# Filter planes of 289 columns loaded in long runs with the negation on VectorE, the first two gate and up chunks split into token halves, and the second block's norms moved into the down stage

## The chip, the cores and the metric

One core of a Trainium2 chip. The metric is the device time of one execution in microseconds (us). "Span" is the length of the profiled execution, which in most runs is some 1.8 us shorter than its time. Engines: PE is TensorE's matmul, PEld its weight load, DVE is VectorE, ACT is ScalarE, POOL is GpSimd, SP is SyncE, which issues most transfers.

## The reference, cut to what matters

```python
x = A_x                                            # 2048 tokens x 576, bf16
X = rfft2(layernorm(x)) * (w_r + 1j * w_i)         # filter planes w_r, w_i: 2048 x 289
h = x + irfft2(X).astype(bf16)
n = layernorm(h)
out = h + (gelu(n @ w_gate) * (n @ w_up)) @ w_down # 576 -> 4608 -> 576
```

The transforms are done as matrix products with tables. The tokens are worked on in 16 tiles of 128; the feed-forward part takes four blocks of four tiles. A "chunk" is 128 of the 4608 hidden columns; each has 18 matmuls of 512 tokens (gate and up).

## The kernel before: what the change and the argument touch

The two filter planes come in 36 loads, 32 of them of 16 partitions, all of one plane first. GpSimd makes the negated imaginary plane, then clears VR. VectorE multiplies the spectrum YS by both planes at once.

```python
def w_loads(pl, hf, eng):                    # column 0 of 289 is skipped: runs of 288
    ...
    for jj in range(4):
        o.append((WS[jj:64:4, g0:g1, 1 + pl, :], 1 + (16 * jj + g0) * K2, [[128 * K2, 16], [K2, g1 - g0], [1, K2 - 1]], jj))
        ...
for f in w_loads(1, 0, SP) + w_loads(1, 1, SP) + w_loads(0, 0, SP) + w_loads(0, 1, SP):
    f()
...
for i in range(NG):                          # 16 pieces of 288 columns on GpSimd
    P.op(POOL, lambda v, g=GORD[i]: v.tensor_scalar(WS[:, g, 0, :], WS[:, g, 2, :], -1.0, 1.0, ...), ...)
    if i == NVZ:
        P.op(POOL, lambda g: g.memset(VR[:, :, :, :, :], 0.0), w=["Vz"])
...
P.op(DVE, lambda v: v.tensor_tensor(TP[:, sl, :, :, q0:q1], y4, w4, op=ALU.mult), ...)   # the product
```

The last eight token tiles are inverse transformed late, inside the down stage of block 0 ("deferred tiles"). One such tile is a matmul group, an eviction EB on ScalarE, four VectorE operations (QB, YB), two matmuls on YB, and then:

```python
def def_n(c):
    for h in range(2):
        P.op(PE, ... ITD[:, c - NPRE, :], YB[:, 288 * h:288 * h + 288] ...)
    P.op(DVE, ... scalar_tensor_tensor(x2, banks(4, 2, 288), 1.0, x2, ..., accum_out=SB2[:, 0, c:c + 1]), ...)  # update of XO
    square(c, JD[:, :], "JD")                # ScalarE, sum of squares for the norm

def down(tb, p):
    for h, (d0, d1) in enumerate(((0, cut), (cut, D))):
        cd = NPRE + 2 * p + h if tb == 0 else NT
        if cd < NT:
            def_i(cd)                        # a deferred tile every 36 matmuls
        for f in ...:
            if cd < NT and f == 22:
                def_n(cd)
            ... matmul of down ...
```

The statistics, norms and DMA transposes of token block 1 are emitted during gate and up of block 0:

```python
if tb == 0 and f == 8:
    ln2_m(2); ln2_r(2); ln2_q(2); ln2_c(2)   # mean, variance, square root, reciprocal
f0, f1 = (15, 3) if tb == 0 else (2, 4)
if tb < 3 and f >= f0 and (f - f0) % f1 == 0 and (f - f0) // f1 < 4:
    norm(...); turn_dma(...)
```

## Time and profile before

| | before |
|---|---|
| time, 3 runs ahead of the prediction | 496.44 us (496.36 to 496.98) |
| span of the profiled run | 494.9 us |
| filter stage, first matmul to first inverse matmul | 19.98 to 52.44 us |
| gate and up of block 0 start | 64.77 us |
| down of block 0 starts (first deferred tile's matmul) | 134.81 us |
| gate and up of block 1 start | 176.16 us |

Read it by stages: from 64.77 us on PE has no gap worth a name, so the time can only fall by what is won ahead of that point, and any new wait after it is paid in full. The prediction shows the profile lines for this. (Its table cuts the down stage at 134.88 us, at the stage's second matmul; below I count from the first, at 134.81.)

### The profile page before, as it was taken

Reading aid. Unit: us, or ns where it says so; the run is one execution under the profiler, and the core shown is the slowest. Engines: PE = TensorE matmul, PEld = TensorE weight load, DVE = VectorE, ACT = ScalarE, POOL = GpSimd, SP = SyncE. Lnnn points to the kernel's source line nnn. Section 1 sums busy time; section 2 is a strip of 40 time slices with the busy share of each in tenths; the row PEclk is TensorE's granted clock in tenths of the full one; section 3 lists DMA queues with packets and bytes.
Section 4 is the critical chain, followed back from the end, with each engine's and each line's share of the span. In section 5 each row is a group of like instructions: output and inputs, shape, how many; then the busy total and the mean of one; then the engine's idle time right before and its main releaser. Section 6 shows DMA issues by size and latency. Waiting matters only on the chain.

```text
span 494.9 us, 9880 instructions
## 1 busy us (share of the span) xinstructions
PE 486.1 (98%) x4338; PEld 288.1 (58%) x4338; DVE 192.4 (39%) x418; ACT 158.9 (32%) x300; POOL 34.6 (7%) x53
## 2 busy tenths in 40 slices
PE   7999999999999999999999999999999999999998
PEld 3767655555588854444477744444677544444775
DVE  6679743444365644433311144333211233333111
ACT  6989865232312243232300033232100132233000
POOL 5750701000000010000000000000000000000000
DMA  8666898411000062000000001000000000000000
GB/s 276 163 188 215 277 350 275 178 25 27 4 13 13 19 191 60 19 9 1 1 13 19 18 15 23 19 1 1 7 19 12 14 1 1 1 1 2 12 19 19
DMA packets 27164, 31.26 MB, mean 63 GB/s; under 512 B 11664, under 2 KB 20112, under 8 KB 27120
## 3 DMA queue, kind: packets, MB, share of 16 engines
q1 hardware_dynamic: 24224, 18.68, 13.0%
q0 software_dynamic: 2896, 11.95, 7.1%
q8 instruction: 34, 0.56, 0.5%
q14 instruction: 10, 0.08, 0.1%
HBM read 26.28 MB, written 2.36 MB: 58 GB/s over the span
## 4 chain that ended last, share of the span: by engine, by line
PE 88%; DVE 4%; issue 1%; ACT 0%; DVEq 0%
PE PS L824 57%; PE PS L874 29%; DVE TP L594 1%; DVE VR L565 1%; PE PS L841 1%; PE PS L684 1%; PE PS L723 1%; DVE ZS L600 1%; DVE XO L726 0%; PE PS L855 0%; DVE ZR L603 0%; PE PS L610 0%; DVE HN L757 0%; PE PS L777 0%; DVE TM L734 0%
## 5 line engine op out<-in xcount | busy, mean ns | idle before, releaser
L824 PE MATMUL PS<-HT,WG 64*128 64x512 bf16 x2106 | 228.5, 376 | 0.0
L824 PEld LDWEIGHTS PS<-HT,WG 64*128 64x128 bf16 x2106 | 107.3, 94 | 119.8 <-issue 1.0
L833 ACT ACTIVATE GL<-PS 128x512 bf16<-128x512 f32 x144 | 85.9, 597 | 257.3 <-PE PS L824 243.4
L834 DVE TENSOR_TENSOR AT<-GL,PS 128x512 bf16<-128x512 bf16 x144 | 98.9, 687 | 175.0 <-ACT GL L833 175.0
L874 PE MATMUL PS<-WD,AT 128*128 128x288 bf16 (+2 forms) x1152 | 144.3, 286 | 0.0
L874 PEld LDWEIGHTS PS<-WD,AT 128*128 128x128 bf16 x1152 | 110.8, 98 | 30.7 <-ACT GL L833 1.3
L877 DVE TENSOR_TENSOR OS<-PS,XO 128x288 bf16<-128x288 f32 (+2 forms) x32 | 14.6, 457 | 100.3 <-PE PS L874 100.3
L824 PE MATMUL PS<-HT,WGX 64*128 64x512 bf16 x486 | 53.4, 376 | 0.0
L824 PEld LDWEIGHTS PS<-HT,WGX 64*128 64x128 bf16 x486 | 23.7, 94 | 28.8
L714 ACT ACTIVATE JD<-XO 128x576 bf16<-128x576 bf16 x8 | 5.5, 683 | 28.5 <-DVE XO L858 28.5
L594 DVE TENSOR_TENSOR TP<-YS,WS 128x1152 bf16<-128x1152 bf16 (+2 forms) x17 | 11.8, 715 | 6.8 <-DMA WS<-in_A_w_r_dram 6.7
L574 PE MATMUL PS<-FT,U 128*128 128x288 bf16 x96 | 14.1, 286 | 0.1
L565 ACT ACTIVATE CUS<-PS 128x576 bf16<-128x576 f32 x16 | 13.5, 862 | 0.5 <-PE PS L574 0.4
L565 ACT ACTIVATE YS<-PS 128x576 bf16<-128x576 f32 x16 | 11.3, 705 | 2.3 <-DVE TP L594 2.2
L520 PE MATMUL PS<-ATS,XO 128*128 128x128 bf16 (+1 forms) x128 | 10.1, 221 | 1.7 <-POOL XN L534 1.1
L584 PE MATMUL PS<-CUS,BT 128*128 128x288 bf16 x64 | 10.5, 286 | 1.2 <-ACT YS L565 0.9
L464 DVE BATCH_NORM_STATS2 ST<-XO 128x6 f32<-128x288 bf16 x24 | 9.3, 438 | 4.5 <-DMA XO<-in_A_x_dram 4.5
L574 PEld LDWEIGHTS PS<-FT,U 128*128 128x128 bf16 x96 | 9.1, 98 | 2.9 <-ACT CUS L565 0.4
L520 PEld LDWEIGHTS PS<-ATS,XO 128*128 128x128 bf16 (+1 forms) x128 | 7.4, 97 | 4.7 <-POOL XN L534 1.6
L610 PE MATMUL PS<-VT,ZS 128*128 128x256 bf16 x64 | 9.0, 273 | 1.1 <-DVE VR L565 0.5
L565 ACT ACTIVATE V<-PS 128x512 bf16<-128x512 f32 (+1 forms) x17 | 10.0, 639 | 0.3 <-PE PS L610 0.2
L757 DVE TENSOR_SCALAR HN<-XO,TM,RS 128x576 bf16<-128x576 bf16 (+1 forms) x32 | 10.0, 361 | 0.0
(77 smaller groups left out, 215.0 us busy)
## 6 DMA issues: line engine op xcount, KB each, us to landing
WD<-in_B_w_down_dram POOLq DMA_DIRECT2D x9, 576.0 KB, 21.4
WG<-in_B_w_gate_dram POOLq DMA_DIRECT2D x4, 1152.0 KB, 9.7
WG<-in_B_w_up_dram SPq DMA_DIRECT2D x4, 1152.0 KB, 7.9
out_dram<-OS SPq DMA_DIRECT2D x30, 72.0 KB, 1.6
XO<-in_A_x_dram SPq DMA_DIRECT2D x3, 576.0 KB, 7.4
WGX<-in_B_w_gate_dram POOLq DMA_DIRECT2D x1, 1152.0 KB, 6.9
WGX<-in_B_w_up_dram SPq DMA_DIRECT2D x1, 1152.0 KB, 10.8
HT<-HN SPq DMA_TRANSPOSE x60, 2.4
```

What stands on the lines that cost most here:

```text
L464: P.op(DVE, lambda v, c=c, h=h: v.bn_stats(ST1[:, c, h, :], XO[:, c, 288 * h:288 * h + 288]), r=[("X", c)], w=[("ST1", c, h)])
L520: P.op(PE, lambda t, b=b, lhs=lhs, p0=p0, p1=p1, s=s, e=e, o=o, c=c: t.matmul(bank(b, p0, p1, o, o + 128), lhs, ATS[:, c, :], start=s, sto ...
L565: fn = (lambda v: v.tensor_copy(dst, src)) if eng == DVE else (lambda a: a.activation(dst, src, ACTF.Copy))
L574: P.op(PE, lambda t, b=b, m=m, us=us, o=o, g=g: t.matmul(bank(b, 0, 128, 0, 2 * HK), U[:, us, g, :, :], FT[:, 3 * o + (2 if us == 4 else u ...
L584: P.op(PE, lambda t, b=b, tb=tb, m=m, s3=s3, sp_=sp_: t.matmul(bank(b, 0, 128, 0, KW), BT[:, sp_, tb, :], CUS[:, s3, m, :], start=(m == 0) ...
L594: P.op(DVE, lambda v: v.tensor_tensor(TP[:, sl, :, :, q0:q1], y4, w4, op=ALU.mult), r=[("Y", sl), ("Wn", i)] + wkeys[0 if 1 <= g < 9 else ...
L757: P.op(eng, lambda v, c=c, hs=hs, o0=o0, o1=o1, x0=x0, x1=x1: v.tensor_scalar(HN[:, hs, o0:o1], XO[:, c, x0:x1], TM[:, 1, c:c + 1], RS2[:, ...
L824: op = P.op(PE, lambda t, h0=h0, kt=kt, wt=wt, b=b, s=(not second and j == 0), e=(second and j == n - 1): t.matmul(bank(b), wg_tile(slot)[ ...
L833: P.op(ACT, lambda a: a.activation(GL[:, s2, :], bank(b0), ACTF.Gelu_apprx_tanh), r=[("PS", b0)], w=[("GL", s2)])
L834: P.op(DVE, lambda v: v.tensor_tensor(AT[:, f, :], GL[:, s2, :], bank(b0 + 1), op=ALU.mult), r=[("GL", s2), ("PS", b0 + 1)], w=[("AT", f)])
L874: P.op(PE, lambda t, b=b, d0=d0, d1=d1, f=f, p=p: t.matmul(bank(b, 0, 128, 0, d1 - d0), AT[:, f, 128 * p:128 * p + 128], WD[:, f, d0:d1], ...
L877: P.op(DVE, lambda v, b=b, d0=d0, d1=d1, p=p, c=c: v.tensor_tensor(OS[:, p % 2, d0:d1], bank(b, 0, 128, 0, d1 - d0), XO[:, c, d0:d1], op=A ...
```

## The change

Its intent: start the filter products earlier (fewer and longer loads, both first halves ahead of the second halves, negation taken off GpSimd), and fill the end of the inverse stage with the first two gate and up chunks, split in two token halves of 256 columns. It also re-deals the evictions of the filter stage between VectorE and ScalarE, and moves the statistics, norms and transposes of block 1 into the down stage of block 0, where the deferred tiles now come every 28 matmuls.

```diff
+    def w_up(pl, hf):                       # one load of 64 partitions, whole runs
+        P.dma(SP, WS[0:64, 1 + pl, g0:g1, :].rearrange("p g k -> p (g k)"), bass.AP(src, g0 * K2, [[128 * K2, 16], [16 * K2, 4], [1, (g1 - g0) * K2]]), ...)
+    def w_down(pl, hf):                     # four loads of 16 partitions, rows of 289
+    for pl in (1, 0):
+        w_up(pl, 0)
+        w_down(pl, 0)
...
+    for pl in (1, 0):
+        w_up(pl, 1)
+        w_down(pl, 1)
...
-        w3 = WS[:, g, :, q0:q1]
+        w3 = WS[:, 1, g, 1 + q0:1 + q1]     # row pitch 289: every second row starts off 4 bytes
...
+    def st_w(i):                            # negation, 4 pieces of 1156 columns
+            P.op(DVE, lambda v, g0=g0, g1=g1: v.tensor_scalar(WS[:, 0, g0:g1, :], WS[:, 2, g0:g1, :], -1.0, None, op0=ALU.mult), ...)
...
-    for i in range(NG):
-        P.op(POOL, ... tensor_scalar(WS[:, g, 0, :], WS[:, g, 2, :], -1.0, 1.0, ...
-        if i == NVZ:
-            P.op(POOL, lambda g: g.memset(VR[:, :, :, :, :], 0.0), w=["Vz"])
+    P.op(POOL, lambda g: g.memset(VR[:, :, :, :, :], 0.0), r=[("ATS", c) for c in range(NT)], w=["Vz"])
...
+    def gu_first(i):
+        for a in range(4):
+            gu_part(a % 2, a > 1, *PARTS[i])        # PARTS = ((0, 256), (256, 512))
...
+    for j, c in enumerate(range(NPRE, NT)):
+        defer(DSTEP * j, def_i, c)                  # DSTEP, DLAG = 28, 24
+        defer(DSTEP * j + DLAG, def_n, c)
+    t2 = DSTEP * (8 - NPRE) + DLAG
+    defer(t2, ln2, 3)
+    for c in range(4, 8):
+        defer(t2 + 12 + DSTEP * (c - 4), turn, c)
...
-            if tb == 0 and f == 8:
-                ln2_m(2) ...
-            f0, f1 = (15, 3) if tb == 0 else (2, 4)
-            if tb < 3 and f >= f0 ...
+            f0, f1 = 2, 4
+            if 0 < tb < 3 and f >= f0 ...
```

The order of the filter stage and of the inverse stage is a string of tokens in the kernel; both strings are new (the inverse one ends "... z2 N7 z3 G0 G1", where G0 and G1 are the two token halves).

## The prediction

> **What bounds the kernel now.** I read the page's busy shares first, then the table by stretches, then the waits and the timelines of the two stages the change touches, and last the chain of work.
>
> ```profile
> PE 486.1 (98%) x4338; PEld 288.1 (58%) x4338; DVE 192.4 (39%) x418; ACT 158.9 (32%) x300; POOL 34.6 (7%) x53
> PE   7999999999999999999999999999999999999998
> ```
> The matmul engine is busy 98% of the span. That is an average, so I cut it by stage:
>
> ```profile
> 20.00:52.44 32.44, 29.66 (x238) 21.75 (x236) 25.10 (x65) 29.23 (x52) 12.00 (x19) 1.00 0.58 171
> 52.44:64.77 12.33, 11.82 (x100) 8.61 (x101) 9.92 (x34) 10.19 (x24) 7.91 (x11) 1.00 1.02 364
> 64.77:134.88 70.11, 70.11 (x649) 36.62 (x650) 27.42 (x51) 26.94 (x46) 1.28 (x2) 1.00 0.42 135
> 134.88:176.16 41.28, 41.28 (x368) 33.51 (x368) 23.66 (x57) 9.99 (x26) 0.00 (x0) 1.00 0.05 14
> ```
> The columns are stretch, length, then busy time of PE, weight load, DVE, ACT, POOL. From 64.77 us on (gate/up, then down of the first token block) PE has no gap: that time only moves if work is added or a wait appears. Only what lies before 64.77 can be won: the filter stage (20.00 to 52.44) and the inverse stage (52.44 to 64.77).
>
> In the filter stage PE's own work is about 27.6 us: 160 matmuls of 288 columns at 0.122 us start to start (six in 0.735 us), 64 of 256 columns at 0.109, ten small ones. So some 4.8 us of its 32.4 are waits. The waits and the timelines name the source:
>
> ```profile
> DVE TP L594 <- DMA WS<-in_A_w_r_dram: 6.7, 1, 6.7
> 18.16 2.40 DVE L529 CAST U<-PS 128x384 bf16<-128x384 f32 x5
> 27.26 1.43 DVE L594 TENSOR_TENSOR TP<-YS,WS 128x1152 bf16<-128x1152 bf16 x2 [6.70 <-DMA WS<-in_A_w_r_dram]
> 6.76 12.71 SPq L218 DMA_DIRECT2D WS<-in_A_w_i_dram  x18
> 19.51 12.57 SPq L218 DMA_DIRECT2D WS<-in_A_w_r_dram  x18
> ```
> VectorE ends its last forward eviction at 20.56 and stands still until 27.26, when the real filter plane lands. SyncE issues 36 filter loads one after another, 0.70 us each; the eighth real one is issued at about 25.1. After 27.26 VectorE runs nearly without gaps until the last filter product is summed at 51.2, and the chain of work runs through it. So the filter stage is a VectorE chain that a late load starts late.
>
> [...] 36 loads of 36 to 72 KB hold SyncE for 25.3 us. [...] With 289 columns and a start at column 1, every second filter row starts off a 4-byte boundary. The trace of before has no such case[...]. [...]
>
> **The change part by part.**
>
> *Loads.* Half of each plane now goes in one load of 64 partitions with long runs, the rest in four. The first half of both planes is 10 loads instead of 16 and comes before the second halves. It is issued from 6.23 us, at up to 0.7 us each to about 13. Bytes: before has moved x, tables and 1.26 MB of filter only when 4.8 MB are through; at the 203 and 272 GB/s of the stretches 0-7 and 7-20 us that is about 19.5 us. So the wait of 6.7 us goes.
>
> *VectorE chain.* It is now first held by data: forward matmuls at 20.0, evictions, second matmul, eviction of YS. By hand with the trace's durations (CUS 0.86, YS 0.70, four matmuls 0.5) the first product starts at 23.9 instead of 27.26: 3.4 us earlier. Work of VectorE from there to the end: 15 products at 0.68 and a split one 0.75 (11.0), 16 pairs of sums at 0.44 (7.0), seven VR casts at 0.43 (3.0), 2.5 V evictions taken over from ScalarE (about 1.6), the second half of the negations. These are 1156 columns; rows of 128 and 576 columns took 0.25 and 0.42 us, so by that slope about 0.65 each, 1.3 here; the first two run while VectorE would wait. Sum 23.9, before 22.7 in 23.9 with gaps. With the same gaps of 1.2 us the inverse stage starts near 49.2, before 52.44: **3.2 us**. ScalarE loses 2 CUS, 1 YS and 2.5 V evictions and gains VR casts, about 25.4 us from 21.07, and PE 27.6 from 20.0: both end before 49, but close, so I expect no more.
>
> *Inverse stage.* Its matmuls are 48 and 32 at 0.122 and 20 at 0.055, 10.9 us in 12.33. The two gate/up chunks cost 3.9 us (18 matmuls at 0.108 each; half as wide and twice as many when split). Before, they came after: 12.33 + 3.9 = 16.2 us. Now the first token half runs while the last two tiles are still being transposed and evicted, and three of four norms are on POOL. I expect 15.4: **0.8 us**.
>
> *Normalisation of block 1.* The second-block norms, their square root and the transposes move from gate/up of block 0, where they were hidden, into its down stage, and the deferred inverse tiles come every 28 matmuls instead of 36. Here is one such tile before:
>
> ```profile
> 138.47 0.76 DVE L858 SCALAR_TENSOR_TENSOR XO<-PS,XO 128x576 bf16<-128x576 f32 x1 [0.59 <-PE PS L855]
> 139.27 0.68 ACT L714 ACTIVATE JD<-XO 128x576 bf16<-128x576 bf16 x1 [3.40 <-DVE XO L858]
> 140.43 0.41 ACT L844 ACTIVATE EB<-PS 128x288 f32<-128x288 f32 x1 [0.39 <-PE PS L841]
> 140.88 0.82 DVE L848 TENSOR_TENSOR QB<-PS,EB 128x288 f32<-128x288 f32 x2 [0.23 <-ACT EB L844]
> 142.11 0.45 DVE L851 TENSOR_TENSOR YB<-QB 128x288 bf16<-128x288 f32 x1
> 143.18 0.41 PE L855 MATMUL PS<-YB,ITD 128*128 128x288 bf16 x2
> 176.15 1.28 ACT L744 ACT_TABLE_LOAD   x1
> ```
> In program order the steps form a ring: update of XO (L858) to square 0.80, square to the next ScalarE operation 0.68, EB to QB 0.45, QB to the end of the second YB 1.68, then the next update 0.49 after it: 4.10 us. Before, PE took 5.16 us per tile and never waited. At 28 matmuls it takes 28 x 0.1225 + 0.75 = 4.18: the slack is 0.08 us. Into that ring come (a) once, after the first tile, the table load (1.28) and square root (0.3) ahead of the next EB: 1.5 us of PE waiting; (b) in three tiles a norm (0.55) and an output eviction (0.38) between YB and the update: 0.93 in place of 0.49 us, less the slack, 0.36 each, 1.1 in all. **PE loses about 2.5 us** here. The transposes (20 at about 1.3 us on SyncE) start some 10 us into the stage of about 44 and end near 40: no wait, with 3 to 4 us to spare.
>
> Sum: -3.2 - 0.8 + 2.5 = -1.5, so 494.9 us.
>
> **The rivals.** *A, the front gain arrives whole and the down stage costs nothing* (492.4): for it speaks that PE had no gap there before and that ScalarE and VectorE are far from full (9.99 and 23.66 of 41.28 us); against it the ring above, which is latency, not load. [...] *C, another wait takes the place of the removed one*: the 1.26 MB land later than 23.9, because the load of x and tables fills the queue (DMA share 0.87 from 7 to 20 us); each microsecond of delay is one of gain lost, up to 496.5 at 2 us. *D, transposes late*: if each took 2 us the second block would wait some 10 us, about 505; the longest landing seen was 5.8 us against a median of 2.4. One in fifty.
>
> **Range and chances.** The front gain may be 2.5 to 5 us, the cost in the down stage 0 to 3.5; A and C mark the ends, which gives 492.2 to 497.2. Two per cent is 9.9 us: there are not 9.9 us of waits ahead of 64.77 to remove, and only D would add as many.
>
> **What would show it.** Right: the first product at about 24 us, with no DMA wait of microseconds ahead of it; the first inverse matmul near 49; the third gate/up chunk (first full-width matmul of 512 columns) near 64.5, before 68.7; products of odd and even rows equally long, about 0.75 us; in the down stage PE waits for YB in the second tile (1.5 us) and in three more, and the stage takes about 43.8 us for 41.28. Wrong: products of two lengths; PE without a gap in that stage (then 492 to 493); or a wait of the first gate/up chunk of block 1 for the transposes.

-3.2 - 0.8 + 2.5 makes -1.5, which takes 496.4 us to 494.9.

## The result, and the profile after

Ratios below are the mean time of one kernel's fast runs over that of the other's fast runs of the same rounds, so not quite the ratio of the medians quoted beside them.

Before 496.55 us (median of 4 runs, 496.36 to 496.98), after **495.90 us** (495.74 to 496.05). Ratio 0.9986, 95% interval 0.9968 to 1.0003: the same within 2%, and a gain of about 0.65 us that the interval does not set apart from none. The control run later, `after_again`, gave 495.91 us beside 496.45 us.

The page of the kernel after, head lines: the busy share of PE is 98% as before, and the slices show no gap either. Such a page cannot tell where a microsecond went.

```profile
span 494.2 us, 9935 instructions
PE 485.8 (98%) x4374; PEld 285.1 (58%) x4374; DVE 193.8 (39%) x421; ACT 153.3 (31%) x300; POOL 31.3 (6%) x43
PE   7999999999989999999999999999999999999998
```

So to the table by stretches of the kernel after (stretch, length, then busy time of PE, weight load, DVE, ACT, POOL, clock, DMA share, GB/s):

```profile
19.78:50.87 31.09, 29.69 (x242) 22.54 (x240) 29.49 (x71) 26.68 (x52) 5.59 (x7) 1.00 0.61 176
50.87:61.88 11.01, 10.81 (x95) 8.25 (x96) 8.66 (x31) 9.39 (x23) 4.58 (x8) 1.00 1.04 369
61.88:131.96 70.08, 70.08 (x686) 33.20 (x685) 23.94 (x38) 25.20 (x45) 7.40 (x11) 1.00 0.39 129
131.96:175.53 43.57, 42.05 (x371) 33.31 (x370) 25.67 (x69) 10.76 (x27) 1.32 (x2) 1.00 0.20 57
```

The second cut, 50.87 us, lies 0.9 us behind the first inverse matmul, so the first two rows are not to be set against those of the prediction's table; the milestones below can be compared. Gate and up (the third row) still have PE busy from end to end. The down stage (the fourth row) does not any more: 42.05 busy of 43.57. By milestones, in us from the span's start:

| milestone | before | after | gained so far |
|---|---|---|---|
| first matmul of the filter stage | 19.98 | 19.78 | 0.20 |
| first filter product | 27.26 | 24.41 | 2.85 |
| first inverse matmul | 52.44 | 49.98 | 2.46 |
| first matmul of the second inverse step | 53.97 | 51.81 | 2.16 |
| first gate and up matmul | 64.77 | 61.88 | 2.89 |
| first matmul of down, block 0 | 134.81 | 131.96 | 2.85 |
| first gate and up matmul, block 1 | 176.16 | 175.53 | 0.63 |

The front won 2.9 us, and the down stage gave 2.2 of them back: 41.35 us became 43.57. The first 0.20 us are not shown to be the change's: the first filter matmul starts at 19.98 us here and at 19.40 in `before_down_new`, which has the same front. Counted from that matmul, the front won 2.7 us.

The timeline of the kernel after around the start of the filter products (start, us, engine, line, operation, count, and in brackets the idle time and its releaser):

```profile
5.70 3.35 SPq L222 DMA_DIRECT2D WS<-in_A_w_i_dram  x5
9.09 3.17 SPq L222 DMA_DIRECT2D WS<-in_A_w_r_dram  x5
...
16.73 4.35 SPq L222 DMA_DIRECT2D WS<-in_A_w_r_dram  x6
...
17.97 2.40 DVE L534 CAST U<-PS 128x384 bf16<-128x384 f32 x5
18.11 3.52 POOL L648 MEMSET VR<- 128x4096 bf16 x1 [0.84 <-DVE ATS L499]
20.29 2.02 DVE L609 TENSOR_SCALAR WS<-WS 128x1156 bf16<-128x1156 bf16 x2
...
24.41 1.43 DVE L604 TENSOR_TENSOR TP<-YS,WS 128x1152 bf16<-128x1152 bf16 x2
```

The first halves of both planes are issued by 12.3 us, and the wait of 6.7 us on a load ahead of the first product is gone: no bracket stands on that line. But the first two negations take 2.02 us together. Drawn singly, the first takes 1.66 us, and one that runs later 0.46. It began at 20.29 us, while GpSimd was still clearing VR (18.11 to 21.63), and it ended 0.3 us after the clearing did.

The products of the kernel after, all instructions of that tile (durations in ns: shortest, median, longest):

```profile
L604 DVE TENSOR_TENSOR TP<-YS,WS x17: 223/755/764, 24.4 to 48.1; 128x1152 bf16<-128x1152 bf16 x15, 128x1024 bf16<-128x1024 bf16 x1, 128x128 bf16<-128x128 bf16 x1
```

There is one length of product, not two: 755 ns in the median and 764 at most, with every second row off a 4-byte boundary; before, with no such row, the median was 750. So the products of two lengths that the prediction lists under "Wrong" did not come.

The timeline of the kernel after in the down stage, from the end of the first deferred tile to the third:

```profile
136.66 0.68 ACT L731 ACTIVATE JD<-XO 128x576 bf16<-128x576 bf16 x1 [3.63 <-DVE XO L879]
137.44 1.28 ACT L761 ACT_TABLE_LOAD   x1
138.73 0.30 ACT L761 ACTIVATE RS<-RS,EPT 128x4 f32<-128x4 f32 x1
138.94 0.39 ACT L865 ACTIVATE EB<-PS 128x288 f32<-128x288 f32 x1
139.36 0.82 DVE L869 TENSOR_TENSOR QB<-PS,EB 128x288 f32<-128x288 f32 x2
...
141.10 0.42 PE L876 MATMUL PS<-YB,ITD 128*128 128x288 bf16 x2 [1.35 <-DVE YB L872]
...
145.37 0.64 DVE L774 TENSOR_SCALAR HN<-XO,TM,RS 128x576 bf16<-128x576 bf16 x2
145.51 0.42 PE L876 MATMUL PS<-YB,ITD 128*128 128x288 bf16 x2
145.91 0.45 DVE L917 TENSOR_TENSOR OS<-PS,XO 128x288 bf16<-128x288 f32 x1
146.28 0.75 DVE L879 SCALAR_TENSOR_TENSOR XO<-PS,XO 128x576 bf16<-128x576 f32 x1
```

ScalarE's operations start here in the order of the program: square (JD) at 136.66 us, table load at 137.44, square root (RS) at 138.73, which is 1.29 us after the load's start, and then, at 138.94, the eviction EB that everything waits for. PE stands at 141.10 until YB comes. The starts of L876 in this run are 135.41, 141.10, 145.51, 149.91, 154.32, 158.51, 162.68 and 166.86 us, that is periods of 5.69, 4.41, 4.40, 4.41, and then 4.17 to 4.19, which is PE's own work (28 x 0.1225 + 0.75 = 4.18). So PE waits 1.5 us once and 0.23 us three times: 2.2 us. The waits of the weight load, which stands idle a little longer than PE, name the same place, in the sum over the run (us in total, times, longest):

```profile
PEld PS L876 <- DVE YB L872: 2.7, 4, 1.7
```

### The profile page after: what moved, and what is told of

The parts are those of the page before. It is cut to its first block, busy times and chain, and to the rows that moved or that the text cites. A ratio compares the mean times of both kernels' runs of the same rounds, so it can differ in the third digit from the quotient of the medians.

```text
span 494.2 us, 9935 instructions
## 1 busy us (share of the span) xinstructions
PE 485.8 (98%) x4374; PEld 285.1 (58%) x4374; DVE 193.8 (39%) x421; ACT 153.3 (31%) x300; POOL 31.3 (6%) x43
## 4 chain that ended last, share of the span: by engine, by line
PE 87%; DVE 8%; ACT 2%; DMA 1%; issue 1%; SPq 0%; DVEq 0%
PE PS L824 57%; PE PS L914 26%; DVE ST L469 1%; DMA XO<-in_A_x_dram 1%; PE PS L701 1%; PE PS L585 1%; DVE TP L604 1%; PE PS L595 1%; DVE U L534 1%; PE PS L740 1%; DVE QB L869 1%; ACT JD L731 1%; DVE XO L879 1%; PE PS L862 0%; DVE ZS L615 0%
## 5 line engine op out<-in xcount | busy, mean ns | idle before, releaser
L824 PE MATMUL PS<-HT,WG 64*128 64x512 bf16 (+1 forms) x2142 | 228.5, 372 | 0.0
L824 PEld LDWEIGHTS PS<-HT,WG 64*128 64x128 bf16 x2142 | 103.9, 94 | 122.9 <-issue 0.7
L576 ACT ACTIVATE YS<-PS 128x576 bf16<-128x576 f32 x15 | 9.7, 662 | 2.5 <-PE PS L595 2.2
L869 DVE TENSOR_TENSOR QB<-PS,EB 128x288 f32<-128x288 f32 x16 | 6.6, 452 | 7.0 <-ACT EB L865 6.8
L576 ACT ACTIVATE CUS<-PS 128x576 bf16<-128x576 f32 x14 | 9.1, 655 | 0.6 <-PE PS L585 0.4
L510 PE MATMUL PS<-ZD 128*128 128x512 bf16 x20 | 7.4, 534 | 1.5 <-POOL ZD L409 1.5
```

The lines of the kernel that those rows point to most:

```text
L576: fn = (lambda v: v.tensor_copy(dst, src)) if eng == DVE else (lambda a: a.activation(dst, src, ACTF.Copy))
L824: op = P.op(PE, lambda t, h0=h0, kt=kt, wt=wt, b=b, s=(not second and j == 0), e=(second and j == n - 1): t.matmul(bank(b, 0, 128, c0, c1) ...
L869: P.op(DVE, lambda v, i=i, op=op: v.tensor_tensor(QB[:, 2 * i:2 * i + 2, :], o2, e2, op=op), r=["EB", ("PS", 3)], w=[f"Q{i}"])
```

## The experiments

Twelve runs were made, one of them the changed kernel again, each timed in five rounds against the kernel before (medians 496.49, 496.39 and 496.45 us in the three groups). All gave correct results. Theory: the front gain is real and smaller than planned, and the down stage loses some 2 us in a ring of dependences that goes through ScalarE and VectorE in program order. Rivals: the loss is VectorE's load and not the order; the front gain comes from something else than the earlier loads.

### The down stage

**down_old**: the changed kernel, with the down stage, norms and transposes of the kernel before.

```diff
-DSTEP, DLAG = 28, 24
+DSTEP, DLAG = 36, 22
-    defer(t2, ln2, 3)
-    for c in range(4, 8):
-        defer(t2 + 12 + DSTEP * (c - 4), turn, c)
+            if tb == 0 and f == 8:
+                ln2(3)
-            f0, f1 = 2, 4
+            f0, f1 = (15, 3) if tb == 0 else (2, 4)
```

> The changed kernel with the second block's statistics, norms and transposes put back into the gate/up stage of the first block, and the deferred tiles every 36 matmuls as before. Ring theory (the 2.3 us lost in the down stage come from the table load and the norms in the ring of the deferred tiles): the down stage goes from 43.57 back to 41.3 us, PE has no wait for YB, total about 493.6 us. Rival (the down stage is longer because something else of the change, such as the front's later weight loads, disturbs it): stays near 43.5, total 495.9.

493.85 us (493.71 to 494.05), ratio to before 0.9948 [0.9935, 0.9960]; it is faster than both kernels. Down of block 0 starts at 131.93 us, as in the changed kernel, and gate and up of block 1 at 173.30: a stage of 41.37 us instead of 43.57, with no wait for YB. The whole loss sits in what was moved there and in the closer spacing, which this run puts back together.

**before_down_new**: the opposite, the kernel before with the new down stage only (DSTEP and DLAG 28 and 24, the square root, norms and transposes of block 1 after its first deferred tile).

> The kernel before with only the down stage of the changed kernel: statistics, norms and transposes of the second block in the down stage, deferred tiles every 28 matmuls. Ring theory: down stage about 43.6 instead of 41.28 and nothing else changed, total about 498.8, clearly slower than before. Rival (the cost needs the changed front): 496.5.

498.61 us (498.36 to 499.16), ratio 1.0046 [1.0034, 1.0058]. The stage runs from 134.29 to 177.87 us, 43.58 us. The loss of 2.2 us does not depend on the front.

**sqrt_early**: the changed kernel with the statistics and the square root of block 1 alone put back into gate and up; norms, transposes and the spacing of 28 stay.

```diff
-    defer(t2, ln2, 3)
+            if tb == 0 and f == 8:
+                ln2(3)
```

> The changed kernel with only the square root of tiles 4 to 7 (its statistics are ready early) put into the gate/up stage; norms and transposes stay in the down stage, deferred tiles every 28 matmuls. Ring theory: the 1.5 us wait of the second deferred tile goes, the three waits of about 0.2 us stay; down stage about 42.1, total about 494.4. Rival (VectorE is simply loaded too much by the norms): the long wait stays, total 495.9.

494.50 us (494.38 to 494.67), ratio 0.9960 [0.9947, 0.9974]. L876 now starts at 135.45, 139.63, 143.95, 148.36, 152.77 and 156.95 us: the long wait is gone, and three of 0.14 to 0.23 us stay. The stage takes 41.97 us, so the table load and the square root cost 1.6 of the 2.2 us, the norms and output evictions the other 0.6.

**square_late**: the changed kernel with one instruction moved: the square of a deferred tile is emitted four matmuls into the next tile, behind that tile's EB, instead of ahead of it. All the work stays in the stage.

```diff
-        square(c, JD[:, :], "JD")
+        defer(DSTEP * (j + 1) + 4, square, c, JD[:, :], "JD")
```

> The changed kernel with the square of each deferred tile emitted after the next tile's EB instead of before it; same work on every engine. Ring theory (ScalarE's order puts the square and the table load between update and EB): the square leaves the ring (0.7 us) and the table load runs ahead of the wait, so the down stage falls to 41.3 to 41.8, total about 493.8. Rival (load of VectorE): the same work in the same time, nothing changes, 495.9.

494.19 us (493.77 to 494.61), ratio 0.9953 [0.9940, 0.9965]. Its timeline:

```profile
132.66 0.41 ACT L865 ACTIVATE EB<-PS 128x288 f32<-128x288 f32 x1
133.09 1.28 ACT L761 ACT_TABLE_LOAD   x1
...
135.45 0.41 PE L876 MATMUL PS<-YB,ITD 128*128 128x288 bf16 x2
...
137.17 0.30 ACT L761 ACTIVATE RS<-RS,EPT 128x4 f32<-128x4 f32 x1 [2.81 <-DVE RS L756]
...
139.63 0.41 PE L876 MATMUL PS<-YB,ITD 128*128 128x288 bf16 x2
```

With no square in front of it, the table load runs in idle time, at 133.09 us, four microseconds ahead of the square root that needs it. L876 then comes every 4.17 or 4.18 us throughout, and the stage takes 41.35 us, exactly that of the kernel before. VectorE still does every norm and eviction there; had its load been the cause, nothing would have changed. The rival falls, and the cause is the order on ScalarE: the square between the update of XO and the next EB closes the ring. Whether the old spacing of 36 matmuls alone, with all the work left in the stage, would also have been enough no run here shows.

**norm_pool**: the changed kernel with the four norms on GpSimd, which shortens VectorE's part of the ring.

```diff
     def turn(c):
-        norm(c)
+        norm(c, POOL)
```

> The changed kernel with the four norms of the second block in the down stage on POOL instead of VectorE. Ring theory: the 1.5 us wait for the table load stays, the three waits of about 0.2 us go; down stage about 42.9, total about 495.2. Rival (load of VectorE is the cause): nearly the whole 2.3 us goes, total about 493.7.

495.79 us (495.56 to 496.08), ratio 0.9987 [0.9974, 0.9999]: I had expected 495.2 and missed. The stage takes 43.34 us. Two of the three short waits are gone, as expected, and the long one stays; but the first short one grew from 0.23 to about 0.4 us. The timeline of this run shows where:

```profile
139.35 6.47 POOL L774 TENSOR_SCALAR HN<-XO,TM,RS 128x576 bf16<-128x576 bf16 x8 [57.10 <-DVE RS L765]
...
144.31 0.95 DVE L871 TENSOR_TENSOR YB<-QB 128x288 bf16<-128x288 f32 x1
```

All of GpSimd's norms run in one go (139.35 to 145.82 us), and one YB beside them took 0.95 us instead of 0.46. The other three YB operations in that stretch took 0.45 to 0.46, so why this one was longer is not shown.

### The front

**loads_old**: the changed kernel with 36 loads, one plane after the other as before (but of 289 columns; the VT table's load moves ahead of them).

```diff
-    for pl in (1, 0):
-        w_up(pl, 0)
-        w_down(pl, 0)
...
+    for pl in (1, 0):
+        w_loads(pl, 0)
+        w_loads(pl, 1)
```

> The changed kernel with the filter planes loaded as before: 36 loads of 16 partitions (289 columns), imaginary plane whole, then real plane, all after VT. Load theory: the first product waits for the real plane until about 27.2 us instead of 24.4; the matmul engine loses what it cannot make up, inverse stage about 2 us later, total about 498. Rival (the front gain comes from sharing evictions between engines, the loads were not the limit): within 0.5 us of the changed kernel, 495.9 to 496.4.

498.04 us (497.23 to 499.14, 6 runs), ratio 1.0035 [1.0022, 1.0047]. The wait for the load is back in its timeline:

```profile
25.61 1.43 DVE L599 TENSOR_TENSOR TP<-YS,WS 128x1152 bf16<-128x1152 bf16 x2 [1.36 <-DMA WS<-in_A_w_r_dram]
```

The first product comes 1.2 us later than with the new loads (25.61 against 24.41), and gate and up start at 63.08 instead of 61.88. That is earlier than the 27.2 us I had expected for the product, and the wait is 1.36 us and not 6.7: VectorE, which now does some of the evictions ahead of the product, is ready for it at 24.25 us and not at 20.56, and the eighth load of the real plane is issued at 23.11 us instead of 24.00. The profiled run was the fastest of the six; the others' spans were 0.4 to 2.0 us longer. So the new loads are worth 1.2 us in the profile and 2.1 in the medians. The run puts number, shape and order of the loads back together; which of them counts it does not tell.

**neg_pool**: the changed kernel with the negation back on GpSimd, in 16 pieces ahead of VR's clearing.

```diff
+    for i in range(NG):
+        P.op(POOL, lambda v, g=GORD[i]: v.tensor_scalar(WS[:, 0, g, :], WS[:, 2, g, :], -1.0, 1.0, ...), ...)
...
-            st_w(i)
```

> The changed kernel with the negation on POOL again (16 pieces, as before), all else as changed. If moving the negation to VectorE was needed for the gain: total about 496.5 or more, because POOL's pieces are late. My theory (the negation was not on the path; the loads were): first product about 23 to 24.4, total within 0.5 us of the changed kernel, 495.4 to 496.2.

498.50 us (497.11 to 498.88), ratio 1.0034 [1.0023, 1.0046]: missed, I had expected no harm. The first product comes at 23.98 us, as expected, but gate and up start at 62.94. The timeline:

```profile
23.48 6.01 POOL L649 TENSOR_SCALAR WS<-WS 128x289 bf16<-128x289 bf16 x8 [1.08 <-DMA WS<-in_A_w_i_dram]
...
27.29 1.90 DVE L604 TENSOR_TENSOR TP<-YS,WS 128x1152 bf16<-128x1152 bf16 x2
```

Eight pieces that GpSimd did in 4.08 us just before (beside evictions out of PSUM) take 6.01 beside VectorE's products, and two products take 1.90 instead of 1.43. In all, three products and four of the sums beside GpSimd's pieces are longer than in the changed kernel, together by 1.45 us. They all lie between the first product, 0.43 us earlier than in the changed kernel, and the fifth, 0.99 later (29.95 against 28.96), and the delay then stays at about 1.0 to the first inverse matmul (51.02 against 49.98). Beside GpSimd's clearing the products were not longer: in the kernel before, VR's clearing (26.65 to 30.17 us) lay beside the first products, and those took 1.43 us for two; so did two in neg_pool itself (at 31.50 us, beside the clearing of 29.55 to 33.07). In the kernel before, GpSimd's pieces ran from 18.39 to 26.6 us, while VectorE mostly waited for its load (20.56 to 27.26), so no product lay beside them. Why pieces and products take longer side by side no run here shows. Once the loads are early, the negation is better off GpSimd, at least in this order of work (495.90 us against 498.50). The profiled run was the fastest of the five (the other spans were 0.7 to 1.8 us longer), and what the others lost besides is not shown.

**memset_late**: the changed kernel with VR's clearing behind the first two negations.

```diff
-    P.op(POOL, lambda g: g.memset(VR[:, :, :, :, :], 0.0), r=[("ATS", c) for c in range(NT)], w=["Vz"])
...
+            if i == 0:
+                P.op(POOL, lambda g: g.memset(VR[:, :, :, :, :], 0.0), r=[("Wn", 0), ("Wn", 4)], w=["Vz"])
```

> The changed kernel with POOL's zeroing of VR (3.5 us) after the first two negations on VectorE instead of beside them. [...] (the first negation took 1.66 us against 0.46 for the same shape later because it waits until POOL's memset ends at 21.6): the first two negations take about 0.46 each, the first product starts about 1.2 us earlier (23.2 instead of 24.4), total 0.3 to 0.8 lower (the matmul engine is nearly the limit of the stage), about 495.4. Rival (the negation is slow because of the loads landing or the odd start of the rows): 1.66 again, total 495.9.

495.94 us (495.52 to 496.15), ratio 0.9991 [0.9978, 1.0004]. The timeline:

```profile
19.86 0.82 DVE L609 TENSOR_SCALAR WS<-WS 128x1156 bf16<-128x1156 bf16 x2
20.74 3.52 POOL L653 MEMSET VR<- 128x4096 bf16 x1 [3.91 <-DVE WS L609]
```

Both negations together take 0.82 us instead of 2.02: the 1.2 us are gone once the clearing runs behind them. With the clearing beside it the first negation had ended at 21.95 us, 0.3 after the clearing (21.63), so it looks like a wait for the clearing's end; what makes it wait is not shown. The stage as a whole gains less, 0.4 us: from the first filter matmul to the second inverse step 31.64 us, against 32.03. And the time does not move at all. In this run, and in the two below that hold the same edit, the time exceeds the span by 2.0 to 2.1 us, against 1.7 to 1.9 in every other run. Something outside the profiled span takes back what the span gains; the runs do not tell what, and I leave it open.

**no_split**: the changed kernel with the first two chunks whole and after the inverse stage.

```diff
-... N6 p0 p3 A0 z2 N7 z3 G0 G1""".split()
+... N6 p0 p3 A0 z2 N7 z3""".split()
```

> The changed kernel, but with the first two gate and up chunks whole and after the inverse stage, as in the kernel before; everything else stays. Theory (the halves placed inside the inverse stage fill its short waits on evictions, worth some 0.7 us): about 496.5 us, and the third full-width chunk of block 0 about 0.6 us later than in the changed kernel (near 66.4 us from the span's start). Rival (the split only moves the same TensorE work and fills nothing): 495.9 us and the third chunk at 65.8 us.

496.60 us (496.36 to 496.94), against 495.91 for the changed kernel in the same group (`after_again`). Down starts at 132.53 us instead of 131.80, 0.73 later. From the second inverse step to gate and up it takes 10.83 us, as before (10.80), against 10.07 when split. Two lines tell what the split fills, the first gate and up matmuls of no_split, then those of the changed kernel:

```profile
62.49 9.87 PE L824 MATMUL PS<-HT,WG 64*128 64x512 bf16 x89 [0.67 <-DVE HT L798]
```

```profile
61.88 10.36 PE L824 MATMUL PS<-HT,WG 64*128 64x256 bf16 x130
```

A whole chunk waits 0.67 us for the eviction of the last normalised tile; the first token half does not need that tile. That is all the split does, and it is worth 0.7 us.

### Combinations

**best1**: down_old with memset_late's edit. **best2**: square_late with memset_late's edit. **after_again**: the changed kernel as control.

> The front of the changed kernel with the down stage of the kernel before (the run down_old, 493.85 us), and in addition VR's clearing on GpSimd put behind the first two negations. If the clearing costs what the first negation waited for it (1.2 us) in part, 493.0 to 493.5 us; if VectorE had that time to spare, as the run memset_late suggests, 493.85 us.

> The changed kernel with the square of each deferred tile put behind the next tile's exponential (the run square_late, 494.19 us) and VR's clearing behind the first two negations. Expected 493.7 to 494.2 us; the down stage's transform matmuls 4.18 us apart throughout, as in square_late.

> The changed kernel itself, as a control of the other three on the same chip: 495.9 us, within 0.2 us.

best1: 493.79 us (493.60 to 493.85), ratio 0.9945 [0.9932, 0.9959]; the best run of all, and not to be told from down_old (493.85). best2: 494.16 us (493.71 to 494.85), ratio 0.9955 [0.9941, 0.9968]. In best2 the down stage took 42.03 us, although its transform matmuls came every 4.18 us as expected. A new wait stood at its end, in the timeline of PE:

```profile
173.40 2.96 PE L825 MATMUL PS<-HT,WG 64*128 64x512 bf16 x25 [0.62 <-DMA HT<-HN]
```

(The "exponential" of the expectation is EB, a plain eviction.) The transposes for block 1 landed 0.62 us late. That is rival D of the prediction, in small: once the stage is 2.2 us shorter, transposes that are issued inside it can land too late. It need not happen: in the profile of square_late, whose down stage is the same, PE did not wait; the median landing of the 20 transposes was 2.3 us in both. down_old, which issues them during gate and up, shows no such wait.

## Why the prediction was right or wrong, point by point

The total was right: 494.9 us told, 495.9 measured, within the range of 492.2 to 497.2. The mechanism was right on both sides. One term of the sum does not follow from its own parts, and others were mis-sized and partly cancel.

- **The front, told as 3.2 + 0.8 = 4.0 us, measured 2.9.** The step that failed is the 3.2 us of the VectorE chain ("the inverse stage starts near 49.2"), and first of all by a slip. Its parts are a first product at 23.9 us, 23.9 us of work and 1.2 us of gaps. They add up to 49.0 us, and that is when the last product is summed, which before was at 51.2. The prediction set it against the first inverse matmul, which before came 1.2 us after that, at 52.44. Set against 51.2, the parts give 2.2 us, and the whole sum -0.5 us or 495.9, which was measured. That it fits so closely is luck, because the parts were off too:
  - The first product came at 24.41 us instead of 23.9, because the negations were counted as work that runs "while VectorE would wait" and GpSimd's clearing beside them was not counted at all; memset_late shows 0.4 us of the stage from it.
  - From there to the last sum it took 24.4 us (to 48.8) instead of the 25.1 of the parts: by the trace VectorE was busy for 23.36 us of that stretch before and for 23.20 after, so its work did not grow by 1.2.
  - The first inverse matmul followed at 49.98 us, 1.2 later as before, but then 0.3 us more went to the last evictions of V and VR: 1.83 us from it to the second inverse step, 1.53 before. So that step gained 2.16 us.
  - The third chunk, told "near 64.5", started at 65.82.
- **The inverse stage, told 0.8, measured 0.73.** Right in size. The reason was told loosely ("the first token half runs while the last two tiles are still being transposed"): both halves run after the last inverse matmul, and only one wait of 0.67 us is filled, as no_split shows.
- **The loads as the cause of the wait of 6.7 us: right.** loads_old brings a wait of 1.36 us back and loses 1.2 to 2.1 us. With the 0.7 us of the split that is 1.9 to 2.8 of the front's 2.7; whether the re-dealt evictions hold a part of it no run here shows. One reading was off: the eighth real load of the kernel before was issued at 24.00 us and not at about 25.1, because most single loads took 0.60 us, and the mean of 0.70 holds two of 1.5 and 1.7. The load that VectorE waited for was the 26th of the 36, which held SyncE for 25.3 us in all.
- **The ring in the down stage, told 2.5 us, measured 2.2.** The wait for table load and square root was told 1.5 and is 1.51. The three short ones were told 0.36 and are 0.23: norm and output eviction put 0.83 us between YB and the update of XO, not 0.93. square_late takes the whole ring away by moving one instruction and thereby shows that it was the order.
- **Rivals.** A (no cost in the down stage): fell; before_down_new shows the cost by itself. B (products of two lengths): fell, one length, 755 ns in the median. C (a transfer takes the place of the removed wait): no such wait in the kernel after. D (transposes late): not in the kernel after, but by 0.62 us in the profile of best2, so "3 to 4 us to spare" is not safe once the stage has lost its 2.2 us of waits.

## What to carry to other kernels

Before work is moved from a long stage into one that runs a short ring of dependences, add up the ring in program order, engine by engine: here a slack of 0.08 us per tile was as good as none, though ScalarE was busy for only 10.76 and VectorE for 25.67 of the stage's 43.57 us. The cheap cure was order and not less work: an operation whose result is needed late (here the square) belongs behind the next operation that the ring waits for (square_late, 494.19 us against 495.90). And when a load comes earlier, look at what had been running unnoticed during the old wait; beside what now starts there both may take longer (in neg_pool two products 1.90 us instead of 1.43, eight of GpSimd's pieces 6.01 instead of 4.08).
